# Linformer attention with a max-out layer on one Trainium2 core: k and q of batch 0 loaded in pieces of four heads instead of two

## The chip, the cores and the metric

The kernel runs on one core of one Trainium2 chip. The core has five engines that work side by side, each with its own list of instructions: TensorE (PE, with the loads of its weights shown as PEld), VectorE (DVE), ScalarE (ACT), GpSimd (POOL) and SyncE (SP). Transfers between the device memory and the on-chip memory are issued by POOL, SP or ACT and carried out by 16 DMA engines. The metric is the time of one execution on the device in microseconds (us); less is better. The times given are medians of several executions.

## The reference

For eight batches of eight heads, k and v (1024 positions of 64 values) are first projected along the positions to 64 rows by E and F. Attention runs over these 64 rows. The heads side by side form rows of 512 values, which pass through a layer that takes the larger of two products and multiplies by a third matrix.

```python
batch, n_heads, seq, head_dim = (8, 8, 1024, 64)     # k_proj = 64
n_tokens, d_model, d_ff = (8192, 512, 1024)

k_proj = np.einsum('ks,bhsd->bhkd', E, k)
v_proj = np.einsum('ks,bhsd->bhkd', F, v)
scores = scale * np.matmul(q, k_proj.transpose(0, 1, 3, 2))
scores = scores - np.max(scores, axis=-1, keepdims=True)
attn = np.exp(scores)
attn = attn / (np.sum(attn, axis=-1, keepdims=True) + 1e-09)
attn_out = np.matmul(attn, v_proj)
x = np.ascontiguousarray(attn_out.transpose(0, 2, 1, 3)).reshape(B * S, H * D)
h1 = x @ w1
h2 = x @ w2
out = np.maximum(h1, h2) @ w_out
```

All inputs and the output are float32.

## The kernel before

**The computation.** The kernel works in float16 on the chip; loads that change the type are issued by POOL (L101, L112, L126, L135, L139). It writes the max-out as `relu(x (w1 - w2)) w_out + x (w2 w_out)`: `step_wd` (L454 to L458) makes the difference wd on DVE in column blocks, `step_w2t` (L460) transposes w2 on PE, and the product of w2 and w_out becomes `m_sb`. The layer for 16 units (eight batches, two halves of the positions) is done by schemes of seven block products (`up_steps` L634, `down_steps` L718). While the layer of one batch runs, the attention of the next is put in between by a table of slots (L922 to L1032).

**The order of the work is written out by hand** (L70): the engines run their instructions as the program lists them. Batch 0 has no earlier work to hide behind. Its attention is listed straight through in L857 to L897: k's projection of heads 0 to 3 (`step_kv`, L192, with the matmuls at L202), its transposition (`step_kpt`, L231, L235), the transposition of q of heads 0 to 3 (`step_qt`, L256, matmuls at L261, copied out at L266), the scores (`step_sc`, L326, matmuls at L290), then the same for heads 4 to 7, then v in two groups of four heads (L882, L889), the weighted sums (`step_at`, L344, L357) and the first pieces of wd (L888, L892). Then come the first matmuls of the layer (`up_slots`, L431, L439). Between these steps `warm` (L146, L149) issues matmuls on a constant tile, whose result nobody reads.

**The loads at the start.** E goes first, half on SP's queue and half on ACT's (L80). All else is issued by POOL, one transfer after another, in this order: k heads 0-1, k 2-3, the identity matrix (made by POOL itself, L117), q 0-1, q 2-3, k 4-5, k 6-7, F (L112), q 4-5, q 6-7, v in four pieces of two heads (L118), then w2 and w1 in column pieces (L124 to L138), w_out (L139), then k, v and q of batch 1 (L900, L905). One k, q or v piece of two heads is 256 KB as written to the chip (512 KB as read): `load` (L100) moves, for every partition and head, 2 KB of float32 into 1 KB of float16.

**Who waits for which load.** A matmul of k's projection takes four heads at once (`rhs=t[w][:, h0 + h : h0 + h + nh, c, :]` with nh = 4), so it needs both pieces. A transposition of q takes one head; `step_qt` goes through four heads in order, two blocks of positions each, so that its first four transposes need only the first of the two pieces. For v, the projection goes through two heads at a time (nh = 2, L196).

**Eight transfers in flight.** The transfers issued by POOL use eight semaphores in turn. An issue first waits for the landing of the transfer that is eight places ahead of it. This wait is set by the framework and is not in the kernel's text; the lists of instructions show it.

Of the kernel before, what the change touches and what calls it, by code (L numbers as in the profile page):

```python
# [16 lines left out]
def kernel(  # L17
# [14 lines left out]
    B, H, S, D = q.shape  # L32
# [67 lines left out]
    def load(t, n, src, b, h0, h1):  # L100
        nc.gpsimd.dma_start(  # L101
            out=t[n][:, h0:h1],
            in_=src[b, h0:h1].rearrange("h (p c) d -> p h c d", c=NC),
        )

    tiles = {b: {} for b in range(B)}
    for n in ("k", "q", "v"):
        alloc(tiles[0], n)
    for h0 in (0, H // 2):
        for n, src in (("k", k), ("q", q)):  # L110
            if (h0, n) == (H // 2, "q"):
                nc.gpsimd.dma_start(out=f_sb[0:KP, :], in_=F)  # L112
            for h in (h0, h0 + H // 4):
                load(tiles[0], n, src, 0, h, h + H // 4)
            if (h0, n) == (0, "k"):
                ident = const.tile([128, 128], FP32)
                make_identity(nc, ident)  # L117
# [891 lines left out]
    for b in range(3, B):  # L1009
        t = tiles[b]  # L1010
        n = 2 * b - 3
# [12 lines left out]
    for i, (new, old) in enumerate(zip([*groups[1:], none], groups)):  # L1024
        n, h = divmod(i + 2, 2)
# [67 lines left out]
```

## Time and profile before

The profile is of one execution. It took 321.96 us; its span, from the first to the last instruction, is 320.2 us.

| | |
|---|---|
| time, median of 4 runs | 322.14 us (321.45 to 322.28) |
| profiled execution | 321.96 us |
| its span | 320.2 us |
| granted clock of TensorE over the span, mean | 0.999 |
| PE busy | 313.4 us, 98% |
| DVE, ACT, POOL busy | 237.1, 209.5, 44.1 us |
| transfers issued by POOL, share of the 16 DMA engines' span | 56.9% |
| k of batch 0: first issue, start of the matmuls on it | 1.24 us, 7.25 us |
| first matmul on wd (L439) | 23.48 us |

How to read the lines that follow in the prediction: a timeline row has the start in us from the span's start, the duration, the engine, the line of the kernel, the operation, what is written and read, the count of instructions merged, and in brackets how long the engine idled before and what ended that. A row of the chain of waits has the start, the duration and what the time went to. A row of a window has its bounds, its length, the busy time of each engine with the number of instructions, the granted clock, the mean busy share of the 16 DMA engines (over 1 when packets overlap) and the GB/s that they moved. A row of a load has what is moved, the issuing engine, the count, the size and the us from issue to landing.

### The profile page before, as it was taken

Reading aid. Unit: us, or ns where it says so; the run is one execution under the profiler, and the core shown is the slowest. Engines: PE = TensorE matmul, PEld = TensorE weight load, DVE = VectorE, ACT = ScalarE, POOL = GpSimd, SP = SyncE. Lnnn points to the kernel's source line nnn. Section 1 sums busy time; section 2 is a strip of 40 time slices with the busy share of each in tenths; the row PEclk is TensorE's granted clock in tenths of the full one; section 3 lists DMA queues with packets and bytes.
Section 4 is the critical chain, followed back from the end, with each engine's and each line's share of the span. In section 5 each row is a group of like instructions: output and inputs, shape, how many; then the busy total and the mean of one; then the engine's idle time right before and its main releaser. Section 6 shows DMA issues by size and latency. Waiting matters only on the chain.

```text
span 320.2 us, 9162 instructions
## 1 busy us (share of the span) xinstructions
PE 313.4 (98%) x3918; PEld 250.9 (78%) x3918; DVE 237.1 (74%) x422; ACT 209.5 (65%) x373; POOL 44.1 (14%) x68
## 2 busy tenths in 40 slices
PE   7979999999999999999999999999999999999996
PEld 3544587878887888878887888878887888888885
DVE  1356799887967796877967796976967696969683
ACT  1376742767776777667776777667777777765541
POOL 8669102003000400011000300040000000000000
PEclk9999999999999999999999999999999999999999
DMA  8999999999979999799999899899969231303024
GB/s 143 198 199 182 194 206 203 207 187 138 207 135 169 173 207 245 202 197 152 227 215 216 163 208 245 202 167 173 236 128 212 52 100 36 100 33 101 33 100 131
DMA packets 76552, 53.01 MB, mean 166 GB/s; under 512 B 29600, under 2 KB 76320, under 8 KB 76512
## 3 DMA queue, kind: packets, MB, share of 16 engines
q0 software_dynamic: 31088, 28.45, 56.9%
q1 hardware_dynamic: 45056, 23.66, 31.5%
q8 instruction: 30, 0.49, 0.6%
q10 hardware_dynamic: 368, 0.33, 0.3%
q14 instruction: 10, 0.08, 0.1%
HBM read 57.15 MB, written 16.78 MB: 231 GB/s over the span
## 4 chain that ended last, share of the span: by engine, by line
PE 91%; DMA 5%; POOL 1%; issue 1%; DVE 0%; DVEq 0%; POOLq 0%
PE mm_ps L745 47%; PE mm_ps L653 27%; PE mm_ps L439 4%; PE att_ps L202 4%; PE att_ps L302 3%; DMA big<-in_moe_w_dram 3%; PE mm_ps L290 2%; DMA k_sb<-in_k_dram 2%; PE mm_ps L541 2%; POOL k_sb L101 1%; PE mm_ps L261 1%; POOL q_sb L101 0%; PE att_ps L464 0%; DVE o_sb L838 0%; PE mm_ps L464 0%
## 5 line engine op out<-in xcount | busy, mean ns | idle before, releaser
L627 ACT COPY p_sb<-mm_ps 128x512 f32<-128x512 f32 x179 | 101.4, 593 | 44.4 <-PE mm_ps L653 27.4
L745 PEld LDWEIGHTS <-big 128*128 128x128 f16 x768 | 73.5, 98 | 12.3 <-issue 3.6
L745 PE MATMUL mm_ps<-T_sb,big 128*128 128x256 f16 x576 | 77.8, 273 | 0.0
L668 DVE TENSOR_TENSOR gt_sb<-mm_ps,p_sb 128x512 f16<-128x512 f32 x56 | 38.5, 687 | 42.9 <-PE mm_ps L653 42.8
L653 PE MATMUL mm_ps<-big,big 128*128 128x256 f16 x336 | 50.4, 273 | 0.0
L653 PEld LDWEIGHTS <-big 128*128 128x128 f16 x448 | 43.8, 98 | 5.2
L745 PE MATMUL mm_ps<-wo_sb,gt_sb 128*128 128x256 f16 x256 | 42.9, 273 | 0.0
L745 PEld LDWEIGHTS <-gt_sb 128*128 128x128 f16 x376 | 35.2, 98 | 8.9 <-issue 5.0
L653 PEld LDWEIGHTS <-wd_sb 128*128 128x128 f16 x336 | 32.9, 98 | 3.8
L653 PE MATMUL mm_ps<-xt_sb,wd_sb 128*128 128x256 f16 x224 | 33.6, 273 | 0.0
L385 ACT ACTIVATE ex_sb<-mm_ps 128x512 f16<-128x512 f32 x50 | 27.2, 596 | 8.8 <-PE att_ps L302 7.5
L414 DVE TENSOR_TENSOR xt_sb<-att_ps,ld_sb 128x1024 f16<-128x1024 f32 x26 | 31.7, 1218 | 0.1
L775 DVE TENSOR_TENSOR o_sb<-mm_ps,p_sb 128x512 f32<-128x512 f32 x32 | 21.9, 684 | 9.5 <-PE mm_ps L745 7.3
L253 POOL COPY junk<-qt_sb 1x1 f16<-1x1 f16 x6 | 1.4, 225 | 174.8 <-DMA qt_sb<-q_sb 174.8
L745 PE MATMUL mm_ps<-m_sb,xt_sb 128*128 128x256 f16 x128 | 24.4, 273 | 0.0
L671 DVE TENSOR_SCALAR gt_sb<-gt_sb 128x512 f16<-128x512 f16 (+1 forms) x60 | 21.5, 359 | 2.1
L714 ACT ACTIVATE gt_sb<-mm_ps 128x512 f16<-128x512 f32 x28 | 16.8, 600 | 9.0 <-PE mm_ps L653 9.0
L613 DVE TENSOR_TENSOR big<-gt_sb 128x1024 f16<-128x1024 f16 x32 | 21.9, 684 | 0.1
L745 PE MATMUL mm_ps<-wo_sb,big 128*128 128x256 f16 x128 | 21.5, 272 | 0.0
L745 PE MATMUL mm_ps<-T_sb,gt_sb 128*128 128x256 f16 x120 | 20.3, 273 | 0.0
L745 PEld LDWEIGHTS <-xt_sb 128*128 128x128 f16 x188 | 18.4, 98 | 2.1
L668 DVE TENSOR_TENSOR gt_sb<-p_sb 128x512 f16<-128x512 f32 x28 | 19.1, 681 | 0.7 <-ACT p_sb L627 0.6
(107 smaller groups left out, 436.1 us busy)
## 6 DMA issues: line engine op xcount, KB each, us to landing
out_dram<-o_sb SPq DMA_DIRECT2D x62, 256.0 KB, 2.8
k_sb<-in_k_dram POOLq DMA_DIRECT2D x7, 1024.0 KB, 10.4
v_sb<-in_v_dram POOLq DMA_DIRECT2D x7, 1024.0 KB, 16.3
q_sb<-in_q_dram POOLq DMA_DIRECT2D x5, 1024.0 KB, 23.3
q_sb<-in_q_dram POOLq DMA_DIRECT2D x4, 512.0 KB, 19.1
big<-in_moe_w_dram POOLq DMA_DIRECT2D x12, 128.0 KB, 6.5
k_sb<-in_k_dram POOLq DMA_DIRECT2D x4, 256.0 KB, 5.7
q_sb<-in_q_dram POOLq DMA_DIRECT2D x4, 256.0 KB, 6.7
```

The costliest lines, as they stand in the source:

```text
L202: nc.tensor.matmul(out=kv_ps[r * KP : (r + 1) * KP, h * D : (h + nh) * D], lhsT=eft[i][:, c, :], rhs=t[w][:, h0 + h : h0 + h + nh, c, :], ...
L385: nc.scalar.activation(out=t["ex", g, j][:, e, :], in_=banks[e], func=ACTF.Exp, scale=scale)
L414: nc.vector.tensor_tensor(out=x_out(t, g, j).rearrange("q z o n -> q o z n"), in0=at_ps.rearrange("q o (z n) -> q o z n", z=2), in1=ld[:, ...
L439: nc.tensor.matmul(out=h_ps, lhsT=wd_sb[:, r, fb * 128 : (fb + 1) * 128], rhs=t["xt"][:, r, :, j * W : (j + 1) * W], start=(r == 0), stop= ...
L613: nc.vector.tensor_tensor(out=S(i), in0=S(0) if x is None else x, in1=y(), op=op)
L627: copy(out=x, in_=bank)
L653: nc.tensor.matmul(out=bank[:, m * W : (m + 1) * W], lhsT=w_[:, n_, (2 * d + m) * 128 : (2 * d + m + 1) * 128], rhs=a[:, n_, :], start=(n ...
L668: nc.vector.tensor_tensor(out=c_blk(j, c), in0=two(x), in1=two(y), op=ALU.add)
L671: nc.vector.tensor_scalar_max(ap, ap, 0.0)
L714: nc.scalar.activation(out=out, in_=in_, func=ACTF.Relu)
L745: nc.tensor.matmul(out=bank[i][:, 0:CH] if two_banks else bank[:, i * CH : (i + 1) * CH], lhsT=a(c)[:, i * 128 : (i + 1) * 128], rhs=w_(c) ...
L775: nc.vector.tensor_tensor(out=o_sb, in0=two(x), in1=two(y), op=ALU.add)
```

## The change

The inner loop that loaded k and q of batch 0 in two pieces of two heads becomes one load of four heads. `H` is 8, so the pieces are heads 0 to 3 and 4 to 7. The order of the loads, F and the identity matrix between them, v's pieces and all else stay as they are. Behind the change each line of the kernel stands one line higher.

```diff
     for h0 in (0, H // 2):
         for n, src in (("k", k), ("q", q)):
             if (h0, n) == (H // 2, "q"):
                 nc.gpsimd.dma_start(out=f_sb[0:KP, :], in_=F)
-            for h in (h0, h0 + H // 4):
-                load(tiles[0], n, src, 0, h, h + H // 4)
+            load(tiles[0], n, src, 0, h0, h0 + H // 2)
             if (h0, n) == (0, "k"):
                 ident = const.tile([128, 128], FP32)
                 make_identity(nc, ident)
```

## The prediction

> **What bounds the kernel now.** I read the page from the top: the profiled execution took 321.96 us, of which 320.2 us are the span and 1.8 us lie around it; the median of the four runs is 322.14 us, 0.18 us above. I forecast a difference, add it to 321.96, and then move the answer by that 0.18.
>
> ```profile
> span 320.2 us, 9162 instructions
> ...
> PE 313.4 (98%) x3918; PEld 250.9 (78%) x3918; DVE 237.1 (74%) x422; ACT 209.5 (65%) x373; POOL 44.1 (14%) x68
> ...
> PE 91%; DMA 5%; POOL 1%; issue 1%; DVE 0%; DVEq 0%; POOLq 0%
> ```
>
> Over the whole span TensorE is the bound, but the change sits in the first 23 us. There the chain of waits reads otherwise:
>
> ```profile
> 5.46 7.03 DMA k_sb<-in_k_dram
> 12.49 0.29 issue
> 12.78 0.71 POOL big L126
> 13.49 0.17 issue
> 13.66 9.24 DMA big<-in_moe_w_dram
> ...
> 23.00 0.44 DVE wd_sb L455
> 23.43 0.05 issue
> 23.48 1.90 PE mm_ps L439 x8
> ```
>
> The chain starts on POOL, passes through transfers and reaches the first subtraction of the weights (L455), which at 23.00 waits for a piece of w1. From 23.48 on PE works almost without a gap to the end. So what moves 23.48 moves the end, one for one, and nothing else can. Which transfers the PE itself waits for is in its timeline (start, duration, line, idle before):
>
> ```profile
> 7.25 1.03 PE L202 MATMUL mm_ps<-k_sb,eft 128*64 128x256 f16 x8 [0.15 <-DMA k_sb<-in_k_dram]
> ...
> 9.47 1.19 PE L261 MATMUL mm_ps<-ident,q_sb 128*128 128x128 f16 x16
> ...
> 15.44 1.08 PE L261 MATMUL mm_ps<-ident,q_sb 128*128 128x128 f16 x16
> ...
> 18.25 1.41 PE L202 MATMUL mm_ps<-v_sb,eft 128*64 128x128 f16 x32 [0.38 <-DMA v_sb<-in_v_dram]
> ...
> 21.63 0.64 PE L202 MATMUL att_ps<-v_sb,eft 128*64 128x128 f16 x16 [0.25 <-DMA v_sb<-in_v_dram]
> ```
>
> It idles 0.15 us for k, 0.38 and 0.25 us for v; DVE then idles 0.38 us for the weights at L455. All of this hangs on one stream of transfers, in the order k, q, k, F, q, v, weights. In windows of 4 us the stream shows (last numbers: clock, DMA share, GB/s):
>
> ```profile
> 3.20:7.20 4.00, 3.89 (x25) 1.73 (x23) 1.08 (x3) 0.00 (x0) 4.00 (x7) 1.00 1.17 182
> 7.20:11.20 4.00, 3.96 (x54) 2.49 (x55) 1.65 (x4) 0.00 (x0) 3.12 (x5) 1.00 1.20 191
> 11.20:15.20 4.00, 3.77 (x68) 2.08 (x52) 1.19 (x3) 2.54 (x3) 2.70 (x4) 1.00 1.22 203
> 15.20:19.20 4.00, 3.32 (x87) 2.18 (x83) 1.58 (x3) 3.46 (x5) 1.58 (x3) 1.00 1.24 206
> 37.00:41.00 4.00, 4.00 (x28) 2.47 (x26) 3.23 (x6) 2.86 (x5) 0.00 (x0) 1.00 1.24 208
> 144.60:148.60 4.00, 4.00 (x73) 3.42 (x50) 1.92 (x3) 3.51 (x7) 1.03 (x2) 1.00 1.07 130
> ```
>
> From 3.2 us the 16 engines are full without a pause. The first k or q packet shows at 3.2 us. The granted clock is 1.00 in all of these rows.
>
> **POOL's issues.** Eight issues become four; data, destinations and order stay. Before, the four pairs take 1.55, 1.43, 1.45 and 1.47 us (POOL's timeline), 5.90 us in all. The nearest issue of four heads is q of batch 2, two of 512 KB at 51.59 us in 1.50 us together, so 0.75 each and 3.00 us for four: 2.9 us less on POOL. It buys nothing by itself, because POOL is far ahead of the transfers:
>
> ```profile
> 8.13 1.48 POOL L101 DMA_DIRECT2D v_sb<-in_v_dram  x2
> ```
>
> ```profile
> v_sb<-in_v_dram POOLq DMA_DIRECT2D x1, 256.0 KB, 10.1
> ```
>
> The first v piece is issued at 8.13 and lands 10.1 us later. The instruction lists show that an issue waits until the transfer eight places ahead of it has landed. Before, that catches the issues from q's last piece on; afterwards from v's last piece on. From the third w2 piece on (issued at 18.50) it is the same pair of transfers in both; of the four weight pieces ahead of it three wait for an earlier landing than now (the first for q of heads 0 to 3, near 9.8, in place of k's last at 12.49) and the fourth for the same. No issue becomes later, and none is what its own landing waits for. Nothing else stands in POOL's queue there but the identity (L117), which gets 0.8 us earlier and feeds a DVE cast that was waiting for it; the next DVE instruction waits for E, so nothing comes of it. Cost 0; the cover is the backlog of 10 us, and without it these 2.9 us would count as a gain.
>
> **The stream.** What does a boundary between two transfers cost? Two pieces of v: issued at 10.06 and 11.43, landed 10.2 us after each, so 1.37 us apart for 256 KB. Whole k and v of batch 1 (1024 KB): issued at 28.18 and 29.05, landed after 15.2 and 19.6 us, 5.27 us apart, or 1.32 us for 256 KB. Three boundaries fewer in a megabyte save 4 x 1.37 - 5.27 = 0.21 us, 0.07 each at the most; the landings are given to 0.1 us, so zero is the other end. I take 0.03, near the middle: four boundaries give -0.12 us to everything from v on (bounds -0.28 and 0).
>
> By the Trainium skill ("DMA: Bandwidth & Descriptors", Anatomy of one DMA) a transfer has a fixed part of about 2.0 us; four fewer in a row would be an estimate of -8 us, to 314. The landings 1.37 us apart are shorter than one such part, so it overlaps here and the rows decide.
>
> **The start of the first load.** No row shows a four-head load into an empty queue. From below: the two-head load at the same place, after which the queue ran at 182 GB/s at once. From above: k of batch 3 with eight heads into an empty queue at 143.00 us, whose first 4 us ran at 130 GB/s: 4 x (1 - 130/182) = 1.14 us lost. The case in hand is nearest to the first: same place, POOL alone, PE and DVE hardly reading. I take +0.05 us, about the spread of the issue rows (0.72 to 0.78).
>
> **The transposes of q.** The PE's list of waits changes here. Before, the first of 16 transposes waits for q's heads 0 and 1, the fifth for heads 2 and 3; afterwards the first waits for all four. At 9.47 the group took 1.19 us against 1.08 at 15.44: it started on two heads and stood 0.11 us for the others, which landed near 9.75 (issued 4.04, 5.7 us). After the change all sixteen start there: end near 9.75 + 1.08 = 10.85 in place of 10.66, +0.2 us for the PE and all behind it (the qt copies, scores, k of heads 4 to 7). That goes into the wait of 0.38 us at 18.25, of which 0.38 - 0.07 - 0.2 = 0.11 us remains. Without that cover it would cost 0.2 us. The second q group is then no wait: its last piece lands at 7.41 + 8.2 = 15.6, when a PE that is 0.2 late arrives.
>
> "Perfetto Trace Analysis" of the Trainium skill (DMA Optimizations) speaks against this change: smaller transfers let some work start sooner. The trace agrees for these four transposes, worth 0.2 us on the PE; by the rule alone the time would be 0.2 us longer.
>
> **Sum.** -0.12 + 0.05 + 0 (q, covered) + 0 (POOL) = -0.07 us: 321.89 beside the profiled 321.96, 322.07 beside the median. I forecast 322.1 us, no change that can be told: I take 0.2% (0.64 us) as the least that a measurement of this kernel can tell. Own range 321.7 to 322.5.
>
> **Rivals.**
>
> *A, slower: the larger first load fills the engines slowly.* Place: k of heads 0 to 3, 3.2 to 7.2 us. For it: every eight-head load into an empty queue starts slowly (130 GB/s at 144.6; 101 at 215.0). Against it: PE, ACT and DVE worked beside those, and wo, k and v queued behind other transfers run at 208. Loss at eight heads 1.14 us; at four heads by proportion (2 of 6 added heads) 0.38. All of it passes to 23.48, since k, v and weights share the queue and all consumers sit at its heels: 322.07 + 0.33 = 322.4 by proportion, 322.02 + 1.14 = 323.2 in full. It decides as slower from a loss of 0.76 us, that is, from 147 GB/s or less in that window.
>
> *B, faster: POOL's issuing is what slows the early stream.* For it: 182, 191, 203, 206 GB/s as POOL's busy time falls from 4.00 to 1.58 us of each 4. At 208 the first three windows would be 0.50 + 0.33 + 0.10 = 0.93 us shorter; half of the issues gone gives 0.46, with the boundaries 0.58: 321.6. Against it: at 51.6 POOL issues all the time and the stream does 199 (51 to 52). Only the whole 0.93 passes 0.64.
>
> *C: q's 0.2 us isn't covered*, if v lands earlier than I think by more than 0.11: 322.2 to 322.3.
>
> *D: the edit is the same stream to the PE*, no boundary cost, no start cost: 322.1, not to be told from the forecast.
>
> **How the numbers follow.** Forecast with D 0.42, all within 0.2%. A 0.40: 0.35 in its slower part, 0.05 below the bound. B 0.14: 0.10 faster than the bound, 0.04 within. C 0.04, within. So faster 0.10, same 0.42 + 0.05 + 0.04 + 0.04 = 0.55, slower 0.35. I weigh A heavily because its row is the only one of a larger load into an empty queue. The range runs from B's 321.6 to A's full price with 0.1 us over it, 323.3.
>
> **What would show it.** Right: four issues of 0.75 us; the first k or q packets near 3.2 us at 180 GB/s or more; k landed and L202 started near 7.25; the first sixteen transposes unbroken (1.08 us), ending near 10.85; the v wait at 18.2 down to about 0.1 us; L455 near 22.93, L439 near 23.41, and from there the same 296.7 us of work. Wrong, A: L202 on k starts after 7.6 and all that follows shifts with it. Wrong, B: the first window above 195 GB/s. If the shift at L439 does not equal the shift of the span, something past 23.5 us moved, and my claim that only the start can matter falls.

## The result, and the profile after

The changed kernel takes 322.82 us (median of 54 executions, 321.48 to 324.98) beside 322.1 us of the kernel before (78 executions, 321.14 to 323.76). The ratio is 1.0024, with a 95% interval of 1.0016 to 1.0032: slower, by 0.7 us. It isn't a fixed amount: 30 of the 54 executions lie above 322.6 us, and 14 of the 78 before; the fastest of the two kernels are 0.34 us apart. The profiled execution took 322.47 us, 0.51 us more than the profiled one before.

From the page of the changed kernel (span; busy time, share of the span and instructions of each engine):

```profile
span 320.7 us, 9157 instructions
PE 313.7 (98%) x3918; PEld 250.9 (78%) x3918; DVE 237.3 (74%) x422; ACT 209.4 (65%) x373; POOL 40.4 (13%) x64
```

POOL has lost 3.7 us of work, and the span is 0.5 us longer. The windows of the changed kernel, with the columns of those shown of before (bounds, length, busy time of PE, PEld, DVE, ACT and POOL, granted clock, DMA share, GB/s):

```profile
3.20:7.20 4.00, 4.00 (x25) 1.81 (x23) 0.87 (x2) 0.00 (x0) 4.00 (x7) 1.00 1.07 149
7.20:11.20 4.00, 3.59 (x39) 2.14 (x38) 0.96 (x3) 0.00 (x0) 1.78 (x3) 1.00 1.23 198
11.20:15.20 4.00, 3.84 (x64) 2.15 (x62) 1.54 (x4) 2.54 (x3) 1.43 (x3) 1.00 1.22 206
15.20:19.20 4.00, 3.69 (x84) 2.13 (x83) 1.92 (x4) 2.85 (x5) 1.31 (x2) 1.00 1.24 205
```

149 GB/s stand where 182 stood, then 198 for 191 and 206 for 203. In KB (GB/s by us): 728 - 596 = 132 fewer in the first window, and 96 fewer by 19.2 us. At 205 GB/s the 96 KB are 0.47 us. The first window in slices of half a us, before and then after:

```profile
3.20:3.70 0.50, 0.50 (x3) 0.23 (x2) 0.23 (x1) 0.00 (x0) 0.50 (x2) 1.00 1.06 174
3.70:4.20 0.50, 0.50 (x3) 0.17 (x2) 0.10 (x1) 0.00 (x0) 0.50 (x2) 1.00 1.25 199
4.20:4.70 0.50, 0.50 (x2) 0.00 (x0) 0.33 (x1) 0.00 (x0) 0.50 (x1) 1.00 1.37 172
```

```profile
3.20:3.70 0.50, 0.50 (x3) 0.22 (x2) 0.00 (x0) 0.00 (x0) 0.50 (x2) 1.00 0.70 66
3.70:4.20 0.50, 0.50 (x3) 0.17 (x2) 0.22 (x1) 0.00 (x0) 0.50 (x2) 1.00 0.76 57
4.20:4.70 0.50, 0.50 (x3) 0.00 (x0) 0.23 (x1) 0.00 (x0) 0.50 (x2) 1.00 1.02 168
```

The first transfers begin in the same slice, but for one us the stream moves 66 and 57 GB/s where 174 and 199 were moved. The three slices miss (545 - 291) x 0.5 = 127 KB, which is nearly the whole loss of the window: 127 KB at 182 GB/s are 0.70 us. This is k of heads 0 to 3 beginning as one load. What comes of it on PE (timeline: start, duration, operation, idle before), and in the chain of waits:

```profile
7.64 1.03 PE L201 MATMUL mm_ps<-k_sb,eft 128*64 128x256 f16 x8 [0.16 <-DMA k_sb<-in_k_dram]
...
10.29 1.07 PE L260 MATMUL mm_ps<-ident,q_sb 128*128 128x128 f16 x16 [0.26 <-DMA q_sb<-in_q_dram]
...
16.07 1.07 PE L260 MATMUL mm_ps<-ident,q_sb 128*128 128x128 f16 x16
...
19.59 0.64 PE L201 MATMUL mm_ps<-v_sb,eft 128*64 128x128 f16 x16 [0.54 <-DMA v_sb<-in_v_dram]
```

```profile
3.43 9.41 DMA k_sb<-in_k_dram
12.84 0.28 issue
13.12 10.35 DMA big<-in_moe_w_dram
...
23.56 0.44 DVE wd_sb L454
24.00 0.05 issue
24.05 1.90 PE mm_ps L438 x8
```

The matmuls on k start 0.39 us later (7.64 for 7.25), the subtraction of the weights and the first matmul on wd 0.56 and 0.57 us later (23.56 for 23.00, 24.05 for 23.48). The chain has the same links as before: a landing of k frees POOL's issue, and the landing of w1's piece frees DVE.

**A second gate.** The landing of v of batch 1 decides too, which I had not seen. In the kernel before, POOL issues this load at 29.05 and it lands 19.6 us later, at 48.65; in the changed one at 29.39, 19.8 us, 49.19. The first matmuls on k and v of batch 1, before and then after:

```profile
48.41 0.40 PE L202 MATMUL att_ps<-k_sb,eft 128*64 128x512 f16 x1
48.72 0.38 PE L202 MATMUL att_ps<-v_sb,eft 128*64 128x512 f16 x1
```

```profile
48.98 0.40 PE L201 MATMUL att_ps<-k_sb,eft 128*64 128x512 f16 x1
49.23 0.38 PE L201 MATMUL att_ps<-v_sb,eft 128*64 128x512 f16 x1
```

Each pair works side by side: where v is there in time, both start together (49.00 and 49.00 in one run below). Here v's starts 0.31 and 0.25 us after k's, within 0.1 us of the landing. The view names no wait, because k's matmul fills it; one run below has it in full. From the start on v the rest of the span is 320.2 - 48.72 = 271.5 us before and 320.7 - 49.23 = 271.5 us after. In all 20 profiles of this study it is 271.4 to 271.6, and in 18 of them v's matmul starts behind k's. So the time is that of the transfer stream from 3.2 us up to this landing, plus work that is always the same, as long as PE itself is not late.

### The profile page after: what moved, and what is told of

It is laid out like the page before. It is cut to its first block, busy times and chain, and to the rows that moved or that the text cites. A ratio compares the mean times of both kernels' runs of the same rounds, so it can differ in the third digit from the quotient of the medians.

```text
span 320.7 us, 9157 instructions
## 1 busy us (share of the span) xinstructions
PE 313.7 (98%) x3918; PEld 250.9 (78%) x3918; DVE 237.3 (74%) x422; ACT 209.4 (65%) x373; POOL 40.4 (13%) x64
## 4 chain that ended last, share of the span: by engine, by line
PE 91%; DMA 6%; POOL 1%; DVE 0%; issue 0%; DVEq 0%; POOLq 0%
PE mm_ps L744 47%; PE mm_ps L652 27%; PE mm_ps L438 4%; PE att_ps L201 4%; DMA big<-in_moe_w_dram 3%; PE att_ps L301 3%; DMA k_sb<-in_k_dram 3%; PE mm_ps L289 2%; PE mm_ps L540 2%; PE mm_ps L260 1%; PE att_ps L463 0%; DVE o_sb L837 0%; PE mm_ps L463 0%; POOL k_sb L101 0%; PE att_ps L289 0%
## 5 line engine op out<-in xcount | busy, mean ns | idle before, releaser
L744 PEld LDWEIGHTS <-gt_sb 128*128 128x128 f16 x376 | 35.2, 98 | 9.0 <-issue 5.0
L384 ACT ACTIVATE ex_sb<-mm_ps 128x512 f16<-128x512 f32 x50 | 27.2, 597 | 8.8 <-PE att_ps L301 7.5
```

The lines of the kernel that those rows point to most:

```text
L384: nc.scalar.activation(out=t["ex", g, j][:, e, :], in_=banks[e], func=ACTF.Exp, scale=scale)
L744: nc.tensor.matmul(out=bank[i][:, 0:CH] if two_banks else bank[:, i * CH : (i + 1) * CH], lhsT=a(c)[:, i * 128 : (i + 1) * 128], rhs=w_(c) ...
```

## The experiments

Each was timed beside the kernel before on the same chip. "Pieces of two heads" are those of the kernel before. A load by halves moves four heads into 64 partitions, so it has as many pieces of 2 KB (256) as a load of two heads; a load of four heads has 512. The diffs are against the kernel before. All of them in one table: median, ratio with its 95% interval, and of the profiled execution the KB moved from 3.2 to 19.2 us (four windows of 4 us, GB/s by us), the GB/s in 27.2 to 31.2 and 31.2 to 35.2 us, the start of the matmuls on v of batch 1, and the span.

| k 0-3, q 0-3, heads 4-7 | median us | ratio | KB by 19.2 | GB/s at 27.2, 31.2 | v of batch 1 | span |
|---|---|---|---|---|---|---|
| before: twos, twos, twos | 322.1 | 1 | 3128 | 179, 170 | 48.72 | 320.2 |
| after: whole, whole, whole | 322.82 | 1.0024 [1.0016, 1.0032] | 3032 | 156, 194 | 49.23 | 320.7 |
| e1: whole, twos, twos | 322.32 | 1.0006 [0.9994, 1.0018] | 2956 | 198, 177 | 48.97 | 320.6 |
| e2: twos, whole, whole | 323.23 | 1.0031 [1.0013, 1.0049] | 3016 | 187, 146 | 50.39 | 321.8 |
| e2 again | 322.69 | 1.0025 [1.0003, 1.0048] | 2968 | 157, 191 | 49.60 | 321.0 |
| f3: twos, whole, twos | 322.36 | 1.0019 [1.0004, 1.0035] | 3012 | 196, 176 | 48.92 | 320.4 |
| e7: twos, twos, whole | 322.49 | 1.0002 [0.9992, 1.0013] | 2960 | 200, 197 | 49.00 | 320.5 |
| e10: halves, halves, halves | 321.96 | 0.9992 [0.9976, 1.0008] | 3116 | 194, 173 | 48.50 | 320.0 |
| e4: halves, whole, whole | 322.12 | 0.9999 [0.9988, 1.0010] | 3088 | 189, 180 | 48.95 | 320.4 |
| e4 again | 322.21 | 0.9996 [0.9982, 1.0011] | 3036 | 193, 174 | 48.79 | 320.2 |
| e4 third | 322.17 | 1.0002 [0.9991, 1.0014] | 3036 | 189, 175 | 48.82 | 320.3 |
| f1: twos, halves, whole | 322.63 | 1.0021 [1.0007, 1.0034] | 3068 | 179, 139 | 50.06 | 321.6 |
| f2: whole, halves, whole | 322.81 | 1.0027 [1.0006, 1.0048] | 2892 | 181, 141 | 50.79 | 322.2 |
| f4: halves, whole, twos | 322.51 | 1.0026 [1.0013, 1.0040] | 2984 | 197, 176 | 49.15 | 320.6 |
| f4 again | 322.27 | 1.0007 [0.9992, 1.0021] | 3068 | 162, 201 | 48.86 | 320.4 |
| e9: twos, twos, twos, q waits for both | 322.01 | 0.9992 [0.9977, 1.0008] | 3092 | 199, 203 | 48.23 | 319.7 |
| e5: after, POOL paused | 323.03 | 1.0029 [1.0015, 1.0042] | 2856 | 203, 201 | 49.17 | 320.6 |
| e8: e2, q issued earlier | 322.64 | 1.0014 [1.0004, 1.0024] | 2892 | 189, 181 | 49.41 | 320.9 |
| e3: k in 1 + 3 heads, whole, whole | 323.00 | 1.0020 [1.0005, 1.0034] | 2968 | 159, 198 | 49.94 | 321.4 |
| e6: k 0-7 in one load, q whole | 326.02 | 1.0123 [1.0110, 1.0136] | 2916 | 186, 183 | 52.63 | 324.1 |

### Does PE's longer wait for q cost, or the stream?

Here only the order of the first four heads' transposes is turned round, so that the first of them waits for the second piece of q, as in the changed kernel. All loads stay as before.

```diff
-        for h in range(nh):
+        for h in (range(nh) if t is not tiles[0] or h0 else reversed(range(nh))):
```

> All loads as in the kernel before; only the first sixteen transposes of q go through the heads from the last to the first, so that the first of them waits for the second q piece, as the PE has to with one load of four heads. Theory wait (the PE's wait for all four heads of q is what makes loads of four slow): 322.4 to 322.9 us. Theory stream (the transfers themselves come later; the PE's 0.2 us goes into its wait for v): the first group starts near 9.8 and is unbroken (1.07 us), the first matmul on wd stays 0.58 us behind the landing of the second weight piece, 322.0 to 322.2 us.

Ratio 0.9992. PE's timeline of this run:

```profile
9.92 1.07 PE L261 MATMUL mm_ps<-ident,q_sb 128*128 128x128 f16 x16
```

The sixteen transposes run unbroken from 9.92 on, beside 9.47 with a stop before, and the time does not move. The wait by itself is free; the loss is in the stream.

### Which load costs: k, q, or those of heads 4 to 7?

First k of heads 0 to 3 alone as one load:

```diff
-            for h in (h0, h0 + H // 4):
-                load(tiles[0], n, src, 0, h, h + H // 4)
+            cuts = (0, 4) if (h0, n) == (0, "k") else (0, 2, 4)
+            for x, y in zip(cuts, cuts[1:]):
+                load(tiles[0], n, src, 0, h0 + x, h0 + y)
```

> Only k of heads 0 to 3 is one load of four heads; the other six pieces of k and q keep two heads. Theory 1 (a first load of twice the size fills the empty queue slowly): the window 3.2 to 7.2 us at 149 GB/s as in the changed kernel (before: 182), the matmuls on k start near 7.6 (before 7.25), the first matmul on wd near 24.0 (before 23.48), time 322.6 to 322.9 us. Theory 2 (POOL's next issues, brought forward, disturb the first load): they come forward by the saved issue here too, but carry two heads, so some 165 GB/s and 322.3 to 322.5. Theory 3 (the PE's wait for four heads of q makes the loss): 182 GB/s and 322.1.

Then the opposite, only k of heads 0 to 3 in twos, run twice, the second time beside other kernels on another chip:

```diff
+            cuts = (0, 2, 4) if (h0, n) == (0, "k") else (0, 4)
```

> The reverse: k of heads 0 to 3 in two loads of two heads, all other k and q in loads of four. Theory 1: the window 3.2 to 7.2 us at 180 GB/s or more, k's matmuls at 7.25, the first matmul on wd at 23.3 to 23.5, time 321.9 to 322.2 us. Theory 2: the large q and k loads are issued from 3.3 us on, so about 150 to 165 GB/s and 322.4 to 322.8. Theory 3: the first sixteen transposes of q unbroken but late, and the wait for v at 18.2 used up: 322.3 to 322.8.

> The kernel with only the first load split, once more beside the next one. If its 323.2 us was its own: 322.8 to 323.4. If it was an accident of that session: 322.0 to 322.4.

Then k and q of heads 0 to 3 in twos (`h0 == 0` as the condition), and only q of heads 0 to 3 whole (`(0, 4) if (h0, n) == (0, "q") else (0, 2, 4)`):

> k and q of heads 0 to 3 in pieces of two heads as before, k and q of heads 4 to 7 in loads of four. Theory size (a load of four heads, 512 packets, is ready for the engines only some 3.3 us after its issue, one of two heads after 2.1 us, and engines that reach it sooner stand still): the first large load is issued near 4.8 us and reached near 9.5, so nobody stands: 180 GB/s or more in 3.2 to 7.2 us, first matmul on wd at 23.3 to 23.5, 321.9 to 322.2 us. Theory place (only the first load into the empty queue matters, and the slow run with k split and q whole had another cause): the same as that run, 322.8 to 323.6 us.

> Only q of heads 0 to 3 is one load; everything else as before. If q's load alone is the price: 1.002 to 1.003, and a dip of the stream between 6 and 7 us. If it needs the larger loads of heads 4 to 7 behind it: 1.000.

With k alone whole the first window falls to 140 GB/s, further than in the changed kernel, yet the ratio is 1.0006. With k in twos and q whole it is 1.0031 and 1.0025, with q alone whole 1.0019. So my theory that k's first load is the whole price falls: k's alone costs 0.2 us, by its interval at most 0.6 (1.0018), and q's costs as well. In f3 the dip of the stream stands where q's load begins. Its two slices in the kernel before, and then in f3:

```profile
6.20:6.70 0.50, 0.50 (x3) 0.19 (x2) 0.39 (x1) 0.00 (x0) 0.50 (x2) 1.00 1.29 211
6.70:7.20 0.50, 0.39 (x2) 0.00 (x0) 0.00 (x0) 0.00 (x0) 0.50 (x2) 1.00 1.16 190
```

```profile
6.20:6.70 0.50, 0.50 (x3) 0.20 (x2) 0.40 (x1) 0.00 (x0) 0.50 (x1) 1.00 0.58 43
6.70:7.20 0.50, 0.40 (x2) 0.00 (x0) 0.00 (x0) 0.00 (x0) 0.50 (x2) 1.00 0.96 135
```

Larger loads for heads 4 to 7 alone cost nothing that can be told (e7, 1.0002). The chain of waits of e2 shows one way in which a late q reaches the end:

```profile
3.35 8.40 DMA q_sb<-in_q_dram
11.76 0.04 issue
11.80 0.64 PE mm_ps L262 x8
...
24.01 0.63 PE att_ps L303 x32
24.64 1.83 PE mm_ps L440 x8
```

q lands at 11.75, and from 11.80 the chain runs over PE, DVE and ACT to the first matmul on wd (L440) without a transfer; it starts 12.8 us later. In the kernel before, q's last piece landed near 9.75, and 9.75 + 12.8 = 22.55 is 0.9 us ahead of the weights (23.48). So by this estimate a q that is over 0.9 us late takes the place of the weights as the bound of L440. Here it is 2.0 us late. At the end of this run v of batch 1 is late too: its matmul starts 0.22 us behind k's (50.39 and 50.17).

### Is it the number of pieces in a load?

All four groups by halves, 256 pieces in each load, four heads wide as in the changed kernel:

```diff
-            for h in (h0, h0 + H // 4):
-                load(tiles[0], n, src, 0, h, h + H // 4)
+            for p in (0, 64):
+                nc.gpsimd.dma_start(
+                    out=tiles[0][n][p : p + 64, h0 : h0 + H // 2],
+                    in_=src[0, h0 : h0 + H // 2].rearrange("h (p c) d -> p h c d", c=NC)[p : p + 64],
+                )
```

> Eight loads as before, but each with four heads on 64 partitions (the cut that did well for k). Theory stream by packets per load (256 packets as before): 322.0 to 322.2 us, the window 3.2 to 7.2 at 180 GB/s or more. If it is the four heads in one load that slow it: 322.4 to 323. If the cut by partitions is better than the cut by heads in itself: 321.6 to 321.9.

Only k of heads 0 to 3 by halves (the same lines under `if (h0, n) == (0, "k")`), all else whole, three times on three chips:

> k of heads 0 to 3 again in two loads, but cut along the partitions: each has all four heads for 64 partitions; the rest as in the changed kernel. If the number of packets in the first load decides (theory 1 as a matter of size): as with the cut by heads, 180 GB/s or more in 3.2 to 7.2 us and 321.9 to 322.2. If it is the walk over four heads that lie 256 KB apart: 149 GB/s, k's matmuls near 7.6, and 322.6 to 322.9.

> The kernel with the first load cut by partitions and q in one load, once more. If its 322.1 us was its own, although q is one load of four heads: 322.0 to 322.2 and a narrow spread. If q in one load costs by itself: 322.6 to 323.2.

> k of heads 0 to 3 in two loads of 64 partitions, q of heads 0 to 3 and both loads of heads 4 to 7 whole, a third time. If the cut by partitions takes the price away: 1.000. If the first two were chance or a matter of the chip: 1.002.

By halves the time is that of before (0.9992), so four heads in one load are not what costs. There are also eight loads again, so this run alone does not tell the pieces in a load from the number of loads; but e4 with five loads for k and q costs nothing and f3 with seven costs 0.2%, so the number of loads does not order the times. In the column of KB, the three kernels with no load of more than 256 pieces (before, e9, e10) have 3092 to 3128; the seventeen profiles with a larger one have 2856 to 3088, each less than any of the three, though the nearest by 4 KB only. So a load of 512 pieces goes with a slower start in every one of these profiles, by little in some. But whether the time follows is not told by that alone: with k by halves and everything behind it whole it was 0.9999, 0.9996 and 1.0002. Four further cuts were to settle this: q by halves behind k in twos (f1) or behind k whole (f2), heads 4 to 7 whole in both; and k by halves, q whole, heads 4 to 7 in twos (f4, twice).

> k of heads 0 to 3 in two loads of two heads, q of heads 0 to 3 in two loads of 64 partitions and four heads, heads 4 to 7 in one load each. If q's 512 packets in one load were the price of the run with q whole (1.0025 to 1.0031): 1.000, within 0.001. If the price sat in the loads behind q: 1.002 or more again. If two loads by partitions make the stream better than two by heads: below 0.999.

> The changed kernel with q of heads 0 to 3 in two loads of 64 partitions and four heads; k of heads 0 to 3 stays one load. If q's load is the larger part of the price: 1.0005 (as with k whole alone), and the first window of 4 us near 145 GB/s all the same. If k's load is the price: 1.0024 as the changed kernel.

> k of heads 0 to 3 in two loads of 64 partitions and four heads, q of heads 0 to 3 in one load, the rest as before. If the cut of k decides over q's price: 1.000 or less, while f3_only_q is at 1.002 or more. If f3_only_q is at 1.000, so is this, and q's price needs the larger loads behind it. If the earlier result with k in halves was luck of the landings: 1.002 to 1.003 as f3_only_q.

> The same with heads 4 to 7 in loads of two heads, a second time. If whole loads for heads 4 to 7 are what makes the difference: 1.002 to 1.003 again, beside 1.000 of the other. If there is no difference between the two kernels: the same ratio for both, within 0.001.

f1 has 256 pieces in every load of k and q of heads 0 to 3 and costs 0.2% (1.0021), where e7, which differs only in how q is cut, costs nothing that can be told (1.0002; the intervals overlap between 1.0007 and 1.0013). f2 costs as much as the changed kernel though its q is cut. f4 gave 1.0026 and 1.0007 with k by halves, beside 1.0002 of e4 on the same chip as the second. No rule by k's or q's cut fits all of these.

A second place of the stream bears on the time: 27.2 to 35.2 us, where the loads of w_out and of k and v of batch 1 begin, 1024 KB each, the same in all kernels. Its windows in the kernel before, in f1 and in e9:

```profile
27.20:31.20 4.00, 4.00 (x24) 1.88 (x22) 1.48 (x3) 3.40 (x7) 3.71 (x6) 1.00 1.33 179
31.20:35.20 4.00, 4.00 (x32) 2.33 (x31) 2.89 (x5) 3.29 (x5) 1.68 (x2) 1.00 1.18 170
```

```profile
27.20:31.20 4.00, 3.42 (x22) 1.66 (x22) 0.91 (x2) 3.65 (x7) 3.85 (x5) 1.00 1.37 179
31.20:35.20 4.00, 4.00 (x32) 2.25 (x30) 2.64 (x4) 2.33 (x3) 2.62 (x3) 1.00 1.11 139
```

```profile
27.20:31.20 4.00, 4.00 (x21) 1.81 (x19) 1.54 (x3) 3.40 (x7) 3.82 (x5) 1.00 1.38 199
31.20:35.20 4.00, 4.00 (x32) 2.31 (x31) 2.81 (x5) 3.17 (x6) 1.31 (x2) 1.00 1.25 203
```

Here f1 moves 4 x (0 + 31) = 124 KB less than before (0.6 us at 205 GB/s) and e9 4 x (20 + 33) = 212 KB more (1.0 us). f1's profile, only 60 KB behind at 19.2 us, reaches v of batch 1 1.34 us late; e7's, 168 KB behind, makes up 4 x (21 + 27) = 192 KB here, and v waits no longer:

```profile
49.00 0.40 PE L203 MATMUL att_ps<-k_sb,eft 128*64 128x512 f16 x1
49.00 0.40 PE L203 MATMUL att_ps<-v_sb,eft 128*64 128x512 f16 x1
```

In f2, where both places were slow, the wait for v has a line of its own:

```profile
50.16 0.40 PE L208 MATMUL att_ps<-k_sb,eft 128*64 128x512 f16 x1
50.79 0.38 PE L208 MATMUL att_ps<-v_sb,eft 128*64 128x512 f16 x1 [0.22 <-DMA v_sb<-in_v_dram]
```

The three profiles with the latest v, e6 aside (f1, e2, f2: 50.06, 50.39, 50.79), share a late issue. POOL issues w_out in them at 28.40, 29.08 and 29.35, in the other seventeen between 26.90 and 28.14. From 27.2 to 39.2 us they move 112 to 204 KB less than the kernel before, the others from 4 KB less to 224 KB more. The chain of waits of f1 runs over this issue:

```profile
14.58 10.74 DMA big<-in_moe_w_dram
25.32 0.29 issue
25.61 2.79 POOL big L144 x4
28.40 0.89 POOL wo_sb L148
29.29 0.45 POOL k_sb L101
29.74 0.49 issue
30.23 19.79 DMA v_sb<-in_v_dram
```

POOL waits until a piece of the weights has landed at 25.32 and then issues four more pieces, w_out, k and v one behind the other. So v is issued at 30.23 instead of 29.05, which is 1.2 of the 1.34 us; from its issue to its landing it takes 19.8 us, beside 19.6 before and 18.7 to 19.9 in all profiles. At this place POOL is not ahead of the stream. That is read from the profiles; no run changed it to test it.

This place changes from one execution to the next: e2's two profiles have 187, 146 and 157, 191 GB/s in it. Whether a cut at the start changes it on average, by shifting when those issues come, no run separates.

### Does POOL disturb its own loads?

If POOL's next issues slowed the first load, a pause of about 1 us behind the identity should help. It is made of two memsets of a tile that v overwrites later, put into the changed kernel:

```diff
                 make_identity(nc, ident)
+                for h in range(2):
+                    nc.gpsimd.memset(tiles[0]["v"][:, h], 0.0)
```

> The changed kernel, with POOL filling two heads of v's tile with zeros (overwritten by v's load later) between the identity and q's first load, about 1 to 2 us in which it issues nothing. Theory 1: the first load still fills slowly, 149 GB/s (or less, if the queue runs dry before q's load comes) and 322.7 to 323.0. Theory 2: with no issue on top of it the first load runs at 180 GB/s or more, k's matmuls start at 7.25, and 322.0 to 322.3.

The pause took 0.98 us; the ratio is 1.0029 and the first window 134 GB/s. It doesn't help. The other way round, e2 with q issued ahead of the identity:

```diff
-            if (h0, n) == (0, "k"):
+            if (h0, n) == (0, "q"):
                 ident = const.tile([128, 128], FP32)
```

> As the run with only the first load split, but POOL issues q of heads 0 to 3 before it makes the identity, about 0.5 us earlier (2.8 in place of 3.35 us). Theory size: the engines still reach q near 6.2, now 3.4 us after its issue, so the dip of that run (20, 15, 26, 27 packets in fifths of a us in place of 37) goes or shrinks to half; 322.1 to 322.6 us in place of 323.2. Theory place, or a straggling DMA engine that has nothing to do with the lead: 323.0 to 323.5 as there.

Ratio 1.0014, beside 1.0031 and 1.0025 of e2; the intervals overlap, and the KB by 19.2 (2892) are no better. In this profile an issue that is 0.6 us earlier (2.76) did not fill the stream.

### Smaller and larger first loads

k of heads 0 to 3 as one and three heads, `cuts = (0, 1, 4)` for the first k and `(0, 4)` for the rest; and k of all eight heads in one load ahead of q:

> k of heads 0 to 3 as one head and then three; q and the rest in loads of four as in the changed kernel. Theory size: the first piece (128 packets) is ready at once but gone by 3.9 us; the second (384 packets, issued near 2.0) is ready near 4.7, so engines stand between 3.9 and 4.7: 155 to 165 GB/s in 3.2 to 7.2, 322.5 to 323.0 us. Theory place: the first load is small, the queue is no longer empty for the second: 180 GB/s, 322.0 to 322.2 us.

> Dose: k of all eight heads in one load at the start, then q of heads 0 to 3 and 4 to 7 in loads of four (so k's second half comes ahead of q's first: that part is a change of order, about 2.5 us later for q). Theory size: full speed only 4 to 5 us after the issue, 110 to 135 GB/s in 3.2 to 7.2; theory place with a fixed cost for any large first load: 149 GB/s as with four heads. The time has the later q in it, 324 to 327 us by both; the window decides.

One head first doesn't pay for the three behind it (1.0020). With eight heads the first window is at 132 GB/s, and k lands at 11.51 instead of near 7.2; PE waits 4.88 us for it and stays behind to the end. "DMA: Bandwidth & Descriptors" of the Trainium skill (Bandwidth) advises to batch transfers to 1 MiB or more, for at least 75% of the peak rate. That is a rule for the rate. Where PE waits for the first bytes, this kernel's time went the other way: 0.24% lost with k and q in loads of four heads (1 MiB as read), 1.23% with k in one load of eight. In that last run q also comes behind all of k, so the size of the load is only a part of its price.

## Why the prediction was wrong

**The failed step: the start of the larger loads, "+0.05 us" for k and nothing for q.** I bounded k's by 0 (the two-head load at the same place) and 1.14 us (eight heads of batch 3, 130 GB/s) and took a value beside the first, because the place was the same. The size of the load decided instead: the first window fell to 149 GB/s, 0.70 us by the three slices, of which 0.47 us were left at 19.2 us and 0.51 us at v of batch 1. Nor was "by proportion" of rival A (0.38) enough. Rival A had the mechanism and the place of this loss; its point of decision, 147 GB/s, was nearly met, and the measured 0.7 us pass the bound of 0.64 by little. But its "All of it passes to 23.48" does not hold: in e1, with k alone whole, the window moves 168 KB less (0.8 us at 205 GB/s), the first matmul on wd starts only 0.38 us later (23.86), and the ratio is 1.0006. So that 0.70 us in the window and 0.7 us in the time are alike is in part luck. For q my sum had only PE's wait ("0 (q, covered)"), and no rival had more; e2 and f3 show that q's load dips the stream and costs time as well. How the prices of k and q add up in the changed kernel is not shown. A row that differed in size, even one from another place, had to weigh more than the row that shared the place: it was the only one that said anything of the term I was pricing.

**POOL's issues: right.** Three of the four take 0.75 to 0.80 us, and only the first takes 0.89. No run shows a gain from POOL's 3.7 us less; e5 gives 0.98 us of them back without a change that can be told (1.0029 beside 1.0024). "No issue becomes later" was wrong: with the stream late, the fourth piece of the weights is issued at 16.31 instead of 15.93, and v of batch 1 at 29.39 instead of 29.05.

**The stream's boundaries, -0.12 us: not seen.** The windows behind the first are better by 7 and 3 GB/s and worse by 1: 4 x (7 + 3 - 1) = 36 KB, 0.18 us. That fits the bounds of 0 to -0.28, but the same windows scatter by more between runs.

**q's transposes: right, with more cover than I thought.** They ran unbroken (1.07 us), and e9 shows that the wait alone costs nothing. Rival C, that the 0.2 us are uncovered, falls. The cover is not only the 0.38 us wait for v: by the estimate from e2, q may be 0.9 us late before its own chain becomes the bound, as it did there.

**"What moves 23.48 moves the end, and nothing else can": right in the sum, wrong in the reason.** The first matmul on wd moved by 0.57, the span by 0.5. But from that matmul to the end the profiles have 296.2 to 297.7 us (e2, f1 and f2 over 297, those with the late issue), from v of batch 1 on 271.4 to 271.6. The end follows the landing of v of batch 1 whenever PE is in time. By this reading a faster start on wd alone would have won nothing, since PE already stood 0.31 us for v; no run tried it. The chain of waits of the kernel before does not show it, since PE looks busy there; the chains of f1 and f2 do.

**Rival B (POOL slows the stream):** 198 for 191 GB/s with POOL at 1.78 instead of 3.12 us of 4 is in its favour, but e5 and e8 give no time for it. **Rival D (the same stream to PE)** falls with the first window.

**What no term or rival had: the clock.** In 10 of the 54 executions of the changed kernel the mean granted clock is 0.988 to 0.995, and none of these is below 322.77 us. The median of the other 44 is 322.49 us, so some 0.3 of the 0.7 us goes with these ten. Whether the late loads lowered their clock is not shown; the last section has two profiles in which it fell behind a late k.

**Open:** what stands still in the DMA engines while a load of 512 pieces begins; why POOL waits longer for a landing near 25 us in f1, e2 and f2; which cuts of k and q cost on average (f1 against e7, f4 against e4); and whether v of batch 1, loaded earlier, would give the 0.31 us, which was not tried. No version beat the kernel before beyond its interval (the best, e9 and e10, 0.9992, hold 1).

## What to carry to other kernels

Where a stream of transfers has no reserve over its consumers, price the size of the loads at its head before merging them. Here the saved issues bought nothing that a run shows, and larger loads of k and q made the stream begin more slowly and cost 0.24% together. Look for the gate by what stays constant: the start from which the remaining span is the same in all runs shows it, even where the chain of waits names no wait. When a term's price is unknown, a row that differs in the thing that is changed counts for more than a row that shares all the rest.

## What was not expected of the hardware

A late first load can cost TensorE its clock, as the profiles of f2 and e6 show. In f2 PE stood for 1.51 us before k; in e6 for 4.88 us. Windows of f2 and then e6 (the number ahead of the DMA share is the granted clock):

```profile
7.20:8.60 1.40, 0.00 (x0) 0.02 (x1) 0.00 (x0) 0.00 (x0) 0.24 (x1) 0.97 1.21 195
8.60:10.50 1.90, 1.89 (x9) 1.30 (x10) 0.00 (x0) 0.00 (x0) 1.27 (x2) 0.50 1.17 176
10.50:12.20 1.70, 1.70 (x12) 0.57 (x13) 0.71 (x2) 0.00 (x0) 0.63 (x2) 0.58 1.12 170
```

```profile
10.50:12.20 1.70, 0.55 (x3) 0.51 (x4) 0.00 (x0) 0.00 (x0) 0.40 (x1) 0.67 1.17 193
12.20:14.00 1.80, 1.80 (x9) 0.86 (x7) 0.42 (x1) 0.00 (x0) 0.30 (x1) 0.50 1.19 201
```

The clock falls to half behind the idle time, and the eight matmuls on k take 1.89 instead of 1.03 us in both. In e2 an idle time of 1.86 us left the clock at 1.00. "TensorE: Matmul & The Clock Gate" of the Trainium skill (The HAM clock gate) states that the clock drops after an idle window of about 3.4 us, counted in windows that run freely. e6 agrees; in f2 1.51 us of standing were enough, which is less than one such window.

A mean clock of 0.995 over a span of 320 us is what 3.2 us at half the clock make, and f2's profile has this mean. The kernel before had means of 0.995 or less in 9 of the 155 executions beside the experiments, the changed kernel in 10 of 54, and e4, with k by halves, in none of 36. Where in those executions the clock fell is not on record; only the profiles of f2 and e6 show it.
